# Pairs of 64-row products in both halves of a gated MLP's first matrix product

## Chip, cores and metric

The kernel runs on one core of one Trainium2 chip. The metric is the device time of one execution in microseconds. A core has five engines that run their own instruction streams in program order and wait for each other on semaphores: PE (TensorE, matrix products; its weight loads are listed as PEld), DVE (VectorE), ACT (ScalarE), POOL (GpSimd) and SP (SyncE, which here only issues DMA transfers).

## What is computed

A transformer block on 2048 tokens of width 448: attention with 16 heads, then a gated MLP with a spatial mixing matrix. Both are modulated by vectors made from a condition c. The change lies in the product that makes z.

```python
mod = (_silu(c) @ w_mod).reshape(c.shape[0], 6, 1, -1)      # sa, ca, ga, sb, cb, gb
h = _layernorm(x) * (1 + ca) + sa
x = x + ga * attention(h, wqkv, wo)                          # 16 heads
h = _layernorm(x) * (1 + cb) + sb                            # h2 below
z = _gelu(jnp.einsum("bsd,df->bsf", h, w_in))                # 448 -> 1792
z1 = z[..., :896]                                            # first half
z2 = _layernorm(z[..., 896:])                                # second half
g = jnp.einsum("ts,bsf->btf", w_sp, z2) + b_sp[None, :, None]
x = x + gb * jnp.einsum("bsf,fd->bsd", z1 * g, w_out)
```

## The kernel before

**Number format.** Products run in a reduced fp32 format. To keep precision every operand is split in two: a rounded part, "hi", and the rest, "lo". A product of two matrices is hi x hi + lo x hi + hi x lo. With 448 = 3 x 128 + 64 rows to contract, one output tile takes the eleven full products of `STEPS` (L27 to L30): nine for the three whole blocks of 128 rows, and two for the last 64 rows, `STEPS_Z = [(6, 6), (6, 7)]`. In slot 6 of the activations, rows 0 to 63 hold hi of the last 64 rows and rows 64 to 127 hold their lo; slot 6 of the weights holds hi twice. So (6, 6) is hi x hi and lo x hi in one product. (6, 7) is hi x lo: slot 7 of the weights holds lo in rows 0 to 63, and in the first half of z zeros below (the memset of L1135), so half of that product's rows do nothing.

**Activations.** `h2T[g]` is the modulated, transposed input of row group g: 512 tokens, four groups. Group 0 is transposed on TensorE (`h2_first`). For groups 1 to 3, `h2_stats`, `h2_norm` and `h2_turn` (statistics, normalizing and a blockwise transpose on DVE), `h2_put` (four DMAs to memory, `hs_scr`), `h2_load` (five DMAs back: blocks 0, 2, 1, and the last 64 rows twice) and `h2_group` follow. `h2_group` takes one block: an activation with scale and bias on ACT (L1188), a rounding on ACT (L1189) and a subtraction on DVE (helper `sub`, L151).

**First half of z.** `z1_unit(g, f)` (L1197) makes 128 of the 896 columns for one row group: eleven products of 128 x 128 by 512 into one PSUM bank (L1200), a Gelu on ACT into one of four slots of `zbuf` (L1204), and a DMA of the slot to memory (L1205). The loop over g and f has 28 units, counted n = 7g + f. Behind unit n stand, in program order, the steps of `H2_AT` for later row groups: `h2_load(1)` behind n = 0, `h2_group(1)` behind 3, 4 and 5, the statistics to the put of group 2 behind 0 to 3 and of group 3 behind 4 to 7, `h2_load(2)` behind 5, `h2_load(3)` behind 9, `h2_group(2)` behind 8 to 11, `h2_group(3)` behind 13 to 16. Between them stand the loads and splits of the second half's weights (`win_load`, `win_prep`) and, from n = 10 on, the parts of w_out (`wout_load` behind 10 + 2i, `wout_part` behind 12 + 2i, `wout_store` behind 13 + 2i for part i).

**Second half of z.** `z2_gemm(t)` makes one of sixteen token tiles: two times eleven products of 128 x 128 by 448 (L1453), Gelu (L1460), statistics (L1461). `z2_norm` follows one tile later. For tiles 4 to 15 the (6, 7) product is replaced: `z2_halves` (L1437) runs, three times per run, two products of 64 rows, one on rows 0 to 63 from `h2T[g]`, one on rows 64 to 127 from `twin`, a second copy of hi of the last 64 rows in the lower partitions. The two products of a pair belong to the two column halves and go to two banks. `twin_load` fetches the copy from `hs_scr` and `twin_make` (L1430) modulates and rounds it on ACT, once for each of groups 1 to 3.

**What sets the order.** Everything is placed by hand (`manual_schedule`); each engine runs its instructions in the order of the program text. `bank(name)` (L232) hands out PSUM banks in turn from a list of seven. SP issues nearly all DMAs, one after the other; an issue that has to wait holds back those behind it.

Of the kernel before, what the change touches and what calls it, by code (L numbers as in the profile page):

```python
# [99 lines left out]
def tile_adaln_mha_gmlp(ctx, tc, x, wqkv, wo, w_in, w_spT, b_sp, w_out, cT, w_mod0, w_mod, out):  # L100
# [34 lines left out]
    def hview(heap, off, a, b):  # L135
        return heap[:, off : off + a * b].rearrange("p (a b) -> p a b", b=b)
# [13 lines left out]
    def sub(eng, dst, a, hi):  # L150
        eng.tensor_tensor(out=dst, in0=a, in1=hi.bitcast(F32), op=ALU.subtract)  # L151
# [980 lines left out]
    sub(dve, parts[1], osb[h], parts[0])  # L1132
    for g in range(2):
        x_load(g)
    pool.memset(w1[64:128, 7, :].bitcast(F32), 0.0)  # L1135
# [58 lines left out]

    zbuf = []

    def z1_unit(g, f):  # L1197
        ps_t = bank("z1_ps")
        for j, (a, b) in enumerate(STEPS):
            pe.matmul(ps_t, w1[:, b, f * 128 : (f + 1) * 128], h2T[g][:, a, :], start=j == 0, stop=j == NST - 1)  # L1200
# [3 lines left out]
        act.activation(zt, ps_t, AF.Gelu_apprx_tanh)  # L1204
        sp.dma_start(z1_scr[f * 128 : (f + 1) * 128, g * 512 : (g + 1) * 512], zt)  # L1205

    for t in range(8, 12):
        wo_tile(t)
# [18 lines left out]
    def wout_part(f):  # L1227
        raw = wouts[f][0]
        dve.tensor_tensor(out=raw, in0=raw, in1=bcs["gb"], op=ALU.mult)
        hi, lo = (wo3.tile([128, D], F32R, name=f"wout_{i}") for i in range(2))  # L1230
        act.activation(hi, raw, AF.Copy)
        sub(dve, lo, raw, hi)
        wouts[f] = hi, lo
# [78 lines left out]
    def wouts_load(g):  # L1312
        for at_g, i, f in WOUT_AT:
            if at_g == g:
                if (i, f) == (0, 0):
                    tbuf.append(wp.tile([128, 5120], F32R, name="wouts", tag="tw", bufs=1))
                if (i, f) == (1, 4):
                    tbuf.append(wp.tile([128, 1536], F32R, name="wouts2", tag="once", bufs=1))
# [15 lines left out]
    def z_sum(p):  # L1334
        if p >= NM:
            return
        for d, a, b, op in MIX[p][0]:
            if d == ONCE:
                once[:] = [wp.tile([128, 1536], F32, name="once", tag="once", bufs=1).rearrange("p (t c) -> p t c", c=384)]
# [79 lines left out]

    ph4 = ExitStack()  # L1420
    tz = ph4.enter_context(tc.tile_pool(name="tz", bufs=2))
    z_mv = {}

    twins = {}
    twin = wp.tile([128, NG - 1, 512], F32R, name="twin", tag="once", bufs=1)

    def twin_load(g):
        sp.dma_start(twin[64:128, g - 1, :].bitcast(F32), hs_scr[g - 1][384:D, :])

    def twin_make(g):  # L1430
        twins[g] = twin[:, g - 1, :]
        t = twins[g][64:128]
        act.activation(t, t.bitcast(F32), AF.Identity, scale=cols["cb"][64:128, 3:4], bias=cols["sb"][64:128, 3:4])

    z2_ps = {}

    def z2_halves(ts):  # L1437
        for t in ts:
            g, tt = divmod(t, 4)
            cs = slice(tt * 128, (tt + 1) * 128)  # L1440
            for hf, (src, r) in enumerate(((h2T[g][:, 6, :], slice(0, 64)), (twins[g], slice(64, 128)))):
                z2_ps[t, hf] = bank("z2_ps")
                pe.matmul(z2_ps[t, hf][:, :D], src[r, cs], w2[r, 7, hf * D : (hf + 1) * D], start=True, stop=False)

    def z2_gemm(t):
        g, tt = divmod(t, 4)
        st = tz.tile([128, 2, 6], F32, name="stz")
        for hf in range(2):
            early = (t, hf) in z2_ps
            ps_t = z2_ps.pop((t, hf)) if early else bank("z2_ps")  # L1450
            steps = STEPS[:-1] if early else STEPS
            for j, (a, b) in enumerate(steps):
                pe.matmul(  # L1453
                    ps_t[:, :D],
                    h2T[g][:, a, tt * 128 : (tt + 1) * 128],
                    w2[:, b, hf * D : (hf + 1) * D],
                    start=j == 0 and not early,
                    stop=j == len(steps) - 1,
                )
            act.activation(z2[t][:, hf * D : (hf + 1) * D], ps_t[:, :D], AF.Gelu_apprx_tanh)  # L1460
            dve.bn_stats(out=st[:, hf, :], in_=z2[t][:, hf * D : (hf + 1) * D])  # L1461
        mv = tz.tile([128, 2], F32, name="mvz")
        dve.bn_aggr(out=mv, in_=st)
        rs = tz.tile([128, 1], F32, name="rsz")
        rstd_of(mv[:, 1:2], rs, 1)
        z_mv[t] = (mv, rs)
# [245 lines left out]
```

## Time and profile before

| what | value |
|---|---|
| median of 3 runs | 1366.69 us (1366.53 to 1367.1) |
| the profiled execution: its time, its span | 1367.53 us, 1365.7 us |
| first half of z (L1200), on the chain | from 897.49 us, 69.93 us, 308 products |
| second half of z (L1453, L1443), on the chain | from 967.42 us to about 1037.9 us |
| granted TensorE clock | 1.00 throughout |

A page of the profile tells of one execution. Its span runs from the first to the last instruction; the rest of the time lies around it. The chain of waits follows the work that ended last back through what released it. A timeline row is: start, length, engine, line, operation, out<-in, shape, count, and in brackets the idle time of that engine before it and what ended it. The letter q behind an engine (SPq) stands for its sequencer, which issues DMAs. A windows row is: stretch, its length, busy time and count of PE, PEld, DVE, ACT and POOL, granted clock, DMA share, GB/s. In the list of waits a row is: who waited for whom, total us, times, longest.

### The profile page before, as it was taken

The page shows a single profiled execution, that of the slowest core. Times are in us where ns is not written, and L with a number is a line of the kernel's source. Part 1 is how long each engine was busy: PE and PEld are TensorE (multiplying, and loading weights), DVE is VectorE, ACT ScalarE, POOL GpSimd, SP SyncE. Part 2 cuts the span into 40 slices and gives each one's busy share as a digit, 9 for nine tenths or more (in the row PEclk, how much of TensorE's full clock was granted, in tenths as well). Part 3 has the DMA queues.
Part 4 walks back from the last instruction along what each step waited for, and adds up shares of the span by engine and source line. Part 5 has one row for each costly group of instructions (what it writes and reads, how often), then busy time and mean ns, then how long its engine had stood idle before and what let it go on. Part 6 is the DMA issues. An engine that isn't in the chain of part 4 may idle for free.

```text
span 1365.7 us, 20771 instructions
## 1 busy us (share of the span) xinstructions
PE 1359.4 (100%) x7050; PEld 966.1 (71%) x7050; DVE 1112.2 (81%) x1764; ACT 807.3 (59%) x1478; POOL 361.5 (26%) x370
## 2 busy tenths in 40 slices
PE   9999999999999999999999999999999999999998
PEld 7888665556555555555565554888888888888898
DVE  7898999999999999999999991673467778999752
ACT  6623676777677667766776679556335545555411
POOL 2134434244544355654641002210021000000000
PEclk9999999999999999999999999999999999999999
DMA  8465747777677668787873110578604665787553
GB/s 284 139 175 183 229 127 218 232 212 205 216 228 234 178 207 256 216 226 221 239 226 114 43 44 24 184 219 273 234 31 155 226 199 175 259 288 260 177 165 109
DMA packets 144518, 260.59 MB, mean 191 GB/s; under 512 B 22168, under 2 KB 43034, under 8 KB 141866
## 3 DMA queue, kind: packets, MB, share of 16 engines
q1 hardware_dynamic: 141694, 255.09, 60.3%
q10 hardware_dynamic: 2718, 4.19, 0.8%
q8 instruction: 55, 0.90, 0.3%
q14 instruction: 51, 0.42, 0.1%
HBM read 178.07 MB, written 76.34 MB: 186 GB/s over the span
## 4 chain that ended last, share of the span: by engine, by line
PE 99%; DVE 1%; DMA 0%; issue 0%; POOL 0%; ACTq 0%; DVEq 0%
PE st_ps L745 19%; PE mt L713 17%; PE o_ps L760 17%; PE acc L1528 5%; PE acc L1529 5%; PE acc L1530 5%; PE pq L408 5%; PE z_ps L1200 5%; PE z_ps L1453 5%; PE wo_ps L832 3%; PE pv L390 2%; PE y_ps L1599 2%; PE y_ps L1600 2%; PE y_ps L1601 2%; PE acc L1536 1%; PE acc L1537 1%
## 5 line engine op out<-in xcount | busy, mean ns | idle before, releaser
L718 DVE TENSOR_REDUCE pm<-mt 128x1 f32<-128x512 f32 x1024 | 626.1, 677 | 7.9 <-PE mt L713 7.8
L749 ACT ACTIVATE P<-st_ps 128x512 f32<-128x512 f32 x1024 | 512.0, 648 | 201.3 <-PE st_ps L745 197.8
L745 PE MATMUL st_ps<-qst,kst 128*128 128x512 f32 x1024 | 408.3, 408 | 0.0
L713 PE MATMUL mt<-kst,qst 128*128 128x512 f32 x1024 | 401.3, 392 | 0.0
L745 PEld LDWEIGHTS st_ps<-qst,kst 128*128 128x128 f32 x1024 | 191.3, 188 | 127.8 <-DVE pm L718 53.3
L760 PE MATMUL o_ps<-P,V 128*32 128x512 f32 x2048 | 240.0, 597 | 0.0
L713 PEld LDWEIGHTS mt<-kst,qst 128*128 128x128 f32 x1024 | 192.4, 188 | 35.6 <-ACT P L749 1.1
L870 POOL TENSOR_TENSOR ws_raw<-ws_raw 128x512 f32<-128x512 f32 x112 | 144.1, 1291 | 173.2 <-DMA ws_raw<-in_w_spT_dram 107.4
L1414 ACT ACTIVATE heapB<-raw_sp 128x512 fp32r<-128x512 f32 x156 | 96.8, 630 | 98.5 <-PE acc L1530 71.1
L760 PEld LDWEIGHTS o_ps<-P,V 128*32 128x32 f32 x2048 | 58.9, 109 | 127.3 <-issue 90.9
L1530 PE MATMUL acc<-heapB,heapA 128*128 128x512 f32 x312 | 121.4, 389 | 0.0
L1528 PE MATMUL acc<-heapB,heapA 128*128 128x512 f32 x312 | 121.4, 389 | 0.0
L766 DVE TENSOR_TENSOR osb<-osb,o_ps 128x512 f32<-128x512 f32 x82 | 56.3, 687 | 61.9 <-PE o_ps L760 59.9
L151 DVE TENSOR_TENSOR heapB<-raw_sp,heapB 128x512 fp32r<-128x512 f32 x112 | 74.5, 685 | 28.1 <-ACT heapB L1414 28.1
L1529 PE MATMUL acc<-heapB,heapA 128*128 128x512 f32 x222 | 86.5, 390 | 0.0
L1530 PEld LDWEIGHTS acc<-heapB,heapA 128*128 128x128 f32 x312 | 58.6, 188 | 12.2
L1528 PEld LDWEIGHTS acc<-heapB,heapA 128*128 128x128 f32 x312 | 58.6, 188 | 12.1
L408 PE MATMUL pq<-heapD,heapD 128*128 128x512 f32 x196 | 61.8, 390 | 0.0
L151 POOL TENSOR_TENSOR ws_raw<-ws_raw 128x512 fp32r<-128x512 f32 x44 | 56.7, 1289 | 3.5
L786 POOL TENSOR_TENSOR osb<-osb,rb 128x512 f32<-128x512 f32 x15 | 19.3, 1284 | 110.1 <-DMA rb<-r_scr 89.8
L1529 PEld LDWEIGHTS acc<-heapB,heapA 128*128 128x128 f32 x222 | 41.7, 188 | 8.8 <-DVE heapB L151 0.3
L1460 ACT ACTIVATE z<-z_ps 128x448 f32<-128x448 f32 x32 | 17.4, 543 | 45.5 <-PE z_ps L1453 45.5
(230 smaller groups left out, 1661.2 us busy)
## 6 DMA issues: line engine op xcount, KB each, us to landing
ws_raw<-in_w_spT_dram SPq DMA_DIRECT2D x136, 256.0 KB
ws_scr<-ws_raw SPq DMA_DIRECT2D x112, 256.0 KB
ws_raw<-ws_scr SPq DMA_DIRECT2D x88, 256.0 KB
raw_sp<-ws_scr SPq DMA_DIRECT2D x88, 256.0 KB
raw_sp<-in_w_spT_dram SPq DMA_DIRECT2D x68, 256.0 KB
wl_scr<-ws_raw SPq DMA_DIRECT2D x44, 256.0 KB
kst<-qk_scr SPq DMA_DIRECT2D x45, 224.0 KB
qst<-qk_scr SPq DMA_DIRECT2D x45, 224.0 KB
```

Of the source, the lines that this page charges most:

```text
L151: eng.tensor_tensor(out=dst, in0=a, in1=hi.bitcast(F32), op=ALU.subtract)
L408: pe.matmul(pq, wqk[:, b, m * 128 : (m + 1) * 128], hT[g][:, a, :], start=j == 0, stop=j == NST - 1)
L713: pe.matmul(mt, qst[h % 3][:, t * 128 : (t + 1) * 128], kst[h % 3][:, kb * 512 : (kb + 1) * 512], start=True, stop=True)
L718: dve.tensor_reduce(out=pms[h][:, t, kb : kb + 1], in_=mt, axis=AX.X, op=ALU.max)
L745: pe.matmul(st, kst[h % 3][:, kt * 128 : (kt + 1) * 128], qst[h % 3][:, qb * 512 : (qb + 1) * 512], start=True, stop=True)
L749: act.activation(p, st, AF.Exp, scale=SCALE)
L760: pe.matmul(o[32 * qb : 32 * qb + 32, :], V[:, u % NT, h, :], ptiles.pop((u, qb)), start=u == a, stop=u == e - 1)
L870: pool.tensor_tensor(out=a, in0=a, in1=b, op=ALU.add if W_SUMS[v][2] > 0 else ALU.subtract)
L1414: act.activation(hi, raw[0], AF.Copy)
L1528: pe.matmul(o, zh[:, c], hi, start=p < 2 and kt == 0, stop=False, skip_group_check=p > 1)
L1529: pe.matmul(o, zh[:, c], lo, start=False, stop=False, skip_group_check=p > 1)
L1530: pe.matmul(o, zl[:, c], hi, start=False, stop=kt == 3, skip_group_check=p > 1)
```

## The change

Both halves of z now run the (6, 7) product as pairs of 64-row products.

- First half: per row group, units 0 to 3 run ten products each and leave their banks open. Then come three pairs in a row: for units 0 and 1, 2 and 3 (they close their banks), and for 4 and 5 (they open theirs). Four Gelus and four stores follow. Units 4 and 5 run ten products, unit 6 all eleven. To feed the lower rows, lo is kept in all 128 rows of slot 7 of the weights; the memset goes.
- `twin` now holds the copy as finished hi, loaded from `h2T[g]` itself by a DMA ahead of unit 0 of each row group; it has three slots, and group 3 takes that of group 0. The second half uses what is there and loads groups 0 and 3 again; the activations of `twin_make` go.
- Second half: per row group, tiles 0 and 1 run ten products for each half and stay open; then four pairs in a row, for the group's four tiles; then tiles 2 and 3.
- An eighth bank joins the list. `twin` and the later `once` tile live in a pool of their own, and the two w_out tiles have one buffer each instead of two.

```diff
+    tw = ctx.enter_context(tc.tile_pool(name="tw", bufs=1))
+    twin = tw.tile([128, 3, 512], F32R, name="twin", tag="once")
+
+    def twin_load(g):
+        sp.dma_start(twin[64:128, g % 3, :].bitcast(F32), h2T[g][0:64, 6, :].bitcast(F32))
...
-    pool.memset(w1[64:128, 7, :].bitcast(F32), 0.0)
...
-            sub(eng, w1[0:64, 7, :], wraw[0][0:64, 3, :], w1[0:64, 6, :])
+            sub(eng, w1[:, 7, :], wraw[0][:, 3, :], w1[:, 6, :])
...
-    def z1_unit(g, f):
-        ps_t = bank("z1_ps")
-        for j, (a, b) in enumerate(STEPS):
-            pe.matmul(ps_t, w1[:, b, f * 128 : (f + 1) * 128], h2T[g][:, a, :], start=j == 0, stop=j == NST - 1)
+    def z1_halves(g, fs, start):
+        for f, src, r in zip(fs, (h2T[g][:, 6, :], twin[:, g % 3, :]), (slice(0, 64), slice(64, 128))):
+            if start:
+                z1_ps[f] = bank("z1_ps")
+            pe.matmul(z1_ps[f], w1[r, 7, f * 128 : (f + 1) * 128], src[r, :], start=start, stop=not start)
+
+    def z1_act(g, f):
         if not zbuf:
             zbuf.append(t3.tile([128, 4, 512], F32, name="z1t", tag="x3", bufs=3))
         zt = zbuf[0][:, (7 * g + f) % 4, :]
-        act.activation(zt, ps_t, AF.Gelu_apprx_tanh)
+        act.activation(zt, z1_ps.pop(f), AF.Gelu_apprx_tanh)
         sp.dma_start(z1_scr[f * 128 : (f + 1) * 128, g * 512 : (g + 1) * 512], zt)
+
+    def z1_unit(g, f):
+        if f == 0:
+            twin_load(g)
+        z1_mm(g, f, STEPS if f == 6 else STEPS[:-1], f < 4 or f == 6, f > 3)
+        if f == 3:
+            for fs in ((0, 1), (2, 3), (4, 5)):
+                z1_halves(g, fs, fs[0] == 4)
+            for k in range(4):
+                z1_act(g, k)
+        elif f > 3:
+            z1_act(g, f)
...
+    banks.append(7)
...
-        hi, lo = (wo3.tile([128, D], F32R, name=f"wout_{i}") for i in range(2))
+        hi, lo = (wo3.tile([128, D], F32R, name=f"wout_{i}", bufs=1) for i in range(2))
...
-    banks.sort(key=lambda k: k < 3)
-    for g in range(1, NG):
-        twin_load(g)
+    banks.sort(key=lambda k: k > 2)
+    twin_load(0)
     for t in range(NT + 1):
-        if t in (2, 5, 9):
-            twin_make((2, 5, 9).index(t) + 1)
-        if t in (4, 7, 10, 13):
-            z2_halves(range(t, t + 3))
         if t < NT:
-            z2_gemm(t)
-        if 0 < t <= NT:
+            for hf in range(2):
+                z2_mm(t, hf, STEPS[:-1], t % 4 < 2, t % 4 > 1)
+                if t % 4 > 1:
+                    z2_act(t, hf)
+            if t % 4 > 1:
+                z2_stats(t)
+        if t % 4 == 1 and t < NT:
+            for k in range(4):
+                z2_halves(t - 1 + k, k > 1)
+            if t == 1:
+                twin_load(3)
+            for k in range(2):
+                for hf in range(2):
+                    z2_act(t - 1 + k, hf)
+                z2_stats(t - 1 + k)
+                z2_norm(t - 1 + k)
+        if t % 4 == 3 or t % 4 == 0 and t:
             z2_norm(t - 1)
```

`z1_mm` and `z2_mm` issue the listed steps into a unit's or a tile's bank, with start and stop as given; `z2_act` is Gelu and statistics of one half, `z2_stats` the rest of a tile's statistics.

More of the change, by code (lines that the diff above doesn't have):

```diff
@@ L1195, in tile_adaln_mha_gmlp, with z1_mm @@
     zbuf = []
-    def z1_unit(g, f):
-        ps_t = bank("z1_ps")
-        for j, (a, b) in enumerate(STEPS):
-            pe.matmul(ps_t, w1[:, b, f * 128 : (f + 1) * 128], h2T[g][:, a, :], start=j == 0, stop=j == NST - 1)
+    z1_ps = {}
+    def z1_mm(g, f, steps, start, stop):
+        if start:
+            z1_ps[f] = bank("z1_ps")
+        for j, (a, b) in enumerate(steps):
+            pe.matmul(
+                z1_ps[f],
+                w1[:, b, f * 128 : (f + 1) * 128],
+                h2T[g][:, a, :],
+                start=start and j == 0,
+                stop=stop and j == len(steps) - 1,
+            )
+    def z1_halves(g, fs, start):
+        for f, src, r in zip(fs, (h2T[g][:, 6, :], twin[:, g % 3, :]), (slice(0, 64), slice(64, 128))):
+            if start:
+                z1_ps[f] = bank("z1_ps")
+            pe.matmul(z1_ps[f], w1[r, 7, f * 128 : (f + 1) * 128], src[r, :], start=start, stop=not start)
+    def z1_act(g, f):
         if not zbuf:
@@ L1317, in wouts_load @@
                 if (i, f) == (1, 4):
-                    tbuf.append(wp.tile([128, 1536], F32R, name="wouts2", tag="once", bufs=1))
+                    tbuf.append(tw.tile([128, 1536], F32R, name="wouts2", tag="once"))
                 sp.dma_start((wouts_l if i else wouts_h)(f).bitcast(F32), wo2_scr[i, f])
@@ L1421, in tile_adaln_mha_gmlp @@
     tz = ph4.enter_context(tc.tile_pool(name="tz", bufs=2))
[L1422 to L1433, printed above, removed]
-    z2_ps = {}
@@ L1437, in z2_halves @@
[L1437 to L1441, printed above, removed]
-                z2_ps[t, hf] = bank("z2_ps")
[L1443 to L1461, printed above, removed]
@@ new lines, in tile_adaln_mha_gmlp, with z2_mm @@
+    z_mv, z_st = {}, {}
+    z2_ps = {}
+    def z2_mm(t, hf, steps, start, stop):
+        g, tt = divmod(t, 4)
+        ts, fs = slice(tt * 128, (tt + 1) * 128), slice(hf * D, (hf + 1) * D)
+        if start:
+            z2_ps[t, hf] = bank("z2_ps")
+        for j, (a, b) in enumerate(steps):
+            pe.matmul(
+                z2_ps[t, hf][:, :D],
+                h2T[g][:, a, ts],
+                w2[:, b, fs],
+                start=start and j == 0,
+                stop=stop and j == len(steps) - 1,
+            )
@@ new lines, in z2_halves, with z2_act @@
+    def z2_halves(t, start):
+        g, tt = divmod(t, 4)
+        ts = slice(tt * 128, (tt + 1) * 128)
+        for hf, (src, r) in enumerate(((h2T[g][:, 6, :], slice(0, 64)), (twin[:, g % 3, :], slice(64, 128)))):
+            if start:
+                z2_ps[t, hf] = bank("z2_ps")
+            pe.matmul(z2_ps[t, hf][:, :D], src[r, ts], w2[r, 7, hf * D : (hf + 1) * D], start=start, stop=not start)
+    def z2_act(t, hf):
+        if hf == 0:
+            z_st[t] = tz.tile([128, 2, 6], F32, name="stz")
+        o = z2[t][:, hf * D : (hf + 1) * D]
+        act.activation(o, z2_ps.pop((t, hf))[:, :D], AF.Gelu_apprx_tanh)
+        dve.bn_stats(out=z_st[t][:, hf, :], in_=o)
@@ L1462, in z2_gemm, with z2_stats @@
+    def z2_stats(t):
         mv = tz.tile([128, 2], F32, name="mvz")
-        dve.bn_aggr(out=mv, in_=st)
+        dve.bn_aggr(out=mv, in_=z_st.pop(t))
         rs = tz.tile([128, 1], F32, name="rsz")
```

2 lines of the change are left out of this document (1 added, 1 removed).

## The prediction, made before the changed kernel had run

> **What bounds the kernel now.** I read the page first, then busy time by stage, the chain of waits in order of time, and then each engine's timeline across the stage that makes the first half of z.
>
> ```profile
> span 1365.7 us, 20771 instructions
> PE 1359.4 (100%) x7050; PEld 966.1 (71%) x7050; DVE 1112.2 (81%) x1764; ACT 807.3 (59%) x1478; POOL 361.5 (26%) x370
> ...
> PE 99%; DVE 1%; DMA 0%; issue 0%; POOL 0%; ACTq 0%; DVEq 0%
> ```
>
> TensorE is on the chain for 99% of the span. A product that falls away is therefore worth its spacing on TensorE, if nothing else is late there; a wait that TensorE gains is paid in full.
>
> ```profile
> 897.30:967.30 70.00, 70.00 (x310) 57.80 (x310) 35.64 (x67) 38.84 (x63) 2.45 (x2) 1.00 0.87 275
> 967.30:1037.80 70.50, 70.50 (x354) 63.23 (x353) 41.87 (x82) 24.72 (x41) 13.34 (x15) 1.00 0.23 78
> ```
>
> These are the two stages that change, first half of z and second half: length, TensorE busy, its weight loads, DVE, ACT and POOL, then the granted clock (1.00), the DMA share and GB/s. TensorE has no gap in either. The DMA engines differ: 0.87 busy in the first, 0.23 in the second. A transfer that is late has little room to catch up in the first.
>
> ```profile
> 897.49 69.93 PE z_ps L1200 x308
> 967.42 17.83 PE z_ps L1453 x88
> 985.26 0.81 PE z_ps L1443 x6
> 986.06 12.36 PE z_ps L1453 x60
> 998.43 0.81 PE z_ps L1443 x6
> ```
>
> The chain of waits (start, length, count) gives the prices. A full 512-column product costs 69.93/308 = 0.227 us, a 448-column one 17.83/88 = 0.203. Before already has runs of three pairs (L1443). From one run to the next is 998.43 - 985.26 = 13.17 us for 60 full products and 3 pairs. As 63 slots of 0.203 that would be 12.76, so a pair costs one slot, and **going into a run and out of it costs 0.41 us**.
>
> [...]
>
> **The change: what TensorE saves.**
> - Second half: runs stay four, but hold four pairs instead of three. Four slots go: 4 x 0.203 = **-0.81 us**. Ends: 0 if the four added pairs ran one product after the other, -0.81 as in the old runs; I take the latter, since the product form is that of L1443.
> - First half: 28 products of 64 useful rows ran as full ones. 24 become 12 pairs, 12 slots less: 12 x 0.227 = 2.72; four new runs cost 4 x 0.41 = 1.64. **-1.08 us**, 0.27 a row group. The cost of a run with 512 columns isn't in the trace: between nothing (-2.72) and 0.41 x 512/448 = 0.47 (-0.84). I take the 448-column figure, the nearest row.
>
> Together -1.89 us at most, if TensorE waits nowhere.
>
> **What ACT now does later.** Before, each unit's Gelu ran right behind its products. After, the Gelus of units 0 to 3 stand behind the pairs that follow unit 3, four in a row, and h2_group(1) still stands behind them in program order.
>
> ```profile
> 900.08 1.28 ACT L1204 ACT_TABLE_LOAD   x1 [4.79 <-PE z_ps L1200]
> 901.38 0.60 ACT L1204 ACTIVATE z1t<-z_ps 128x512 f32<-128x512 f32 x1
> ...
> 907.52 0.60 ACT L1204 ACTIVATE z1t<-z_ps 128x512 f32<-128x512 f32 x1 [1.89 <-PE z_ps L1200]
> 908.01 0.81 ACT L1188 ACTIVATE hfull<-heapB,col_sb,col_cb 128x512 f32<-128x512 f32 x1
> ...
> 913.92 0.63 ACT L1189 ACTIVATE heapB<-hfull 128x512 fp32r<-128x512 f32 x1
> ...
> 961.65 1.07 ACT L1204 ACTIVATE z1t<-z_ps 128x512 f32<-128x512 f32 x2
> ```
>
> The load of the Gelu table waits for the first unit's products like the Gelu itself (4.79 us idle on PE, then 1.28). Before, it hides behind unit 1. After, the first Gelu waits for 40 products and a pair: 897.49 + 40 x 0.227 + about 0.35 = 906.9. Then 1.28 of table and four Gelus at 0.48 (two take 1.07, so the second starts 0.48 behind the first): h2_group(1) starts at 910.2, not at 908.01. **2.2 us later.** From there to the last block's rounding at 913.92 ACT is without a gap, so all of it shifts.
>
> [...]
>
> ```profile
> 912.74 0.69 DVE L151 TENSOR_TENSOR heapB<-hfull,heapB 128x512 fp32r<-128x512 f32 x1 [1.16 <-ACT heapB L1189]
> ...
> 916.06 0.69 DVE L151 TENSOR_TENSOR heapB<-hfull,heapB 64x512 fp32r<-64x512 f32 x1
> ...
> PEld z_ps L1200 <- DVE heapB L151: 0.2, 1, 0.2
> ```
>
> The last two blocks of h2T[1] are finished by these subtractions; between them DVE does the next group's statistics. The second ends at 916.75, and the (6,6) product of unit (1,0) needs it: due at 897.49 + 77 x 0.227 + 9 x 0.227 = 917.0. The list of waits shows that weight load waiting 0.2 us for it: **no slack at all**. After, it ends 2.2 later and TensorE comes 0.27 sooner: 2.5 us of stall, **S1 = +2.5**. Ends: 1.2 if the table load ran ahead of the wait, 2.5 as the row has it.
>
> **What SP now does later.** SP issues in order. It issues the loads of h2T[3] ahead of the four Gelu stores of group 1, which now come as one batch behind the pairs of (1,3); before, three of those stores were out long before.
>
> ```profile
> 919.03 1.09 SPq L1205 DMA_DIRECT2D z_scr<-z1t  x2
> 921.60 3.68 SPq L1091 DMA_DIRECT2D hs_scr<-turn  x4
> ...
> 929.24 1.27 SPq L1103 DMA_DIRECT2D heap<-hs_scr  x3
> 930.55 1.09 SPq L1105 DMA_DIRECT2D heap<-hs_scr  x2
> 931.69 0.58 SPq L1205 DMA_DIRECT2D z_scr<-z1t  x1
> 932.37 0.38 SPq L1225 DMA_DIRECT2D raw_out<-in_w_out_dram  x1
> ```
>
> ```profile
> 926.06 0.60 ACT L1204 ACTIVATE z1t<-z_ps 128x512 f32<-128x512 f32 x1 [1.16 <-DMA z_scr<-z1t]
> ...
> 928.77 0.57 ACT L1204 ACTIVATE z1t<-z_ps 128x512 f32<-128x512 f32 x1
> ...
> 930.75 0.69 DVE L151 TENSOR_TENSOR heap<-hfull,heap 64x512 fp32r<-64x512 f32 x1 [0.76 <-ACT heap L1189]
> ```
>
> The put of group 3's turned rows is out at 925.28, and its loads start at 929.24: 4.0 us from issue to use. The first of the four stores then goes at 931.69 at the soonest (as does the store there now), or at 933.9 if the whole chain shifts with S1's 2.2. It lands 4.0 us later (by the put; by the store of 919.03, whose slot the Gelu at 926.06 waited for, 7.0). Gelu (1,4) writes the same slot of the four, waits for that landing, and the last block of h2T[2] stands behind it: 928.77 to 931.44 is 2.67 us. So it is ready at 938.4 to 940.6; before, at 931.44. TensorE wants it at 897.49 + 163 x 0.227 - 2 x 0.27 + 2.5 = 936.45; with the 0.2 that S1 showed, the stall is 2.1 to 4.3. **S2 = +3.2**, the middle, since part of the gap from 921.60 to 929.24 is waiting for earlier transfers, which needn't shift. Below, 0, if a store lands at once; above, 7.4 with the 7.0.
>
> ```profile
> 937.81 0.62 DVE L1229 TENSOR_TENSOR raw_out<-raw_out,bc_gb 128x448 f32<-128x448 f32 x1 [6.37 <-DMA raw_out<-in_w_out_dram]
> 938.47 0.58 ACT L1231 ACTIVATE wout<-raw_out 128x448 fp32r<-128x448 f32 x1 [7.27 <-DVE raw_out L1229]
> ```
>
> The copy of h2T[2]'s 64 rows (twin_load(2)) stands on SP behind the stores of the first w_out part. That part's load takes 5.4 us (932.37 to 937.81) and goes three stores later, 933.9 to 936.1. With the product (0.66), rounding (0.6) and two issues (0.9), the copy is issued at 941.5 to 943.7 and lands 4.0 later, 945.5 to 947.7. TensorE wants it at 936.45 + 3.2 + 31 x 0.227 = 946.7: **S3 = +0.5** (0 to 1.0). The copies of groups 0, 1 and 3 I take as covered by the 40 products (9.1 us) ahead of their pairs; if group 1's is late, S2 shrinks by as much.
>
> **Edits at nothing.**
>
> ```profile
> L1135 POOL MEMSET heapA<- x1: 842/842/842, 862.1 to 862.1; 64x896 f32 x1
> L1433 ACT ACTIVATE twin<-twin,col_sb,col_cb x3: 812/812/812, 977.0 to 1008.1; 64x512 fp32r<-64x512 f32 x3
> ```
>
> The memset and the three activations that go are off the chain. Single wout buffers make each rounding on ACT wait for the store before; that puts the last Gelus near 971, while TensorE needs their banks only some 2 us into the second half: covered, about 3 us if not. The eighth bank and the moved `once` cost nothing that these rows show. In the second half ACT is 24.72 us busy of 70.5, and bursts of four Gelus pass.
>
> **Sum.** -0.81 - 1.08 + 2.5 + 3.2 + 0.5 = **+4.3 us**. The profiled execution took 1367.53 (span 1365.7); the median is 1366.69, 0.84 lower. Moved by the same, the time after is 1366.69 + 4.3 = **1371.0**.
>
> **Rivals.**
> - *All of it hidden*: -1.89, **1364.8**, not slower. It needs the (6,6) product of (1,0) not to wait; decided by whether h2_group(1) starts before about 908. For it: TensorE's rows have no gap. Against: the 0.2 us wait. 12%.
> - *S1 alone*: stores land quickly enough that S2 and S3 vanish; 2.5 - 1.89 = +0.6, **1367.3**. Decided by the first store of group 1 landing before 933.5. For: DMA is freed while SP waits for the Gelus. Against: share 0.87, and the 7.0 us of one store. 21%.
> - *ACT becomes the bound*: rounding through single wout buffers runs late by over 3 us, and banks of the last group aren't free when the second half starts; +3 more, **1374 to 1377**. 9%.
> - *Pairs with 512 columns don't overlap*: the first half gains nothing and loses the 1.64; +7.0, 1373.7. Against: L1443 runs as pairs. 2%.
> - *No cost for a run at all*: -2.72 - 0.81 = -3.5, 1363.2. 2%.
>
> The forecast keeps 54%, with 1369.4 to 1374 of its own. A measurement of this kernel can tell about 0.2% (2.7 us) from no change. Faster by more: 0.03 (the last rival, and 1% of the first). Within: 0.34 (the rest of the first, the second, and 2% of the forecast's lower edge). Slower: 0.63 (all else). The range, 1366.0 to 1375.0, leaves out the hidden case, the last rival and the worst of the third.
>
> **What would show it.** TensorE idle at unit (1,0) for DVE's subtraction, 2 to 3 us; a table load near 907; Gelu (1,4) waiting for a DMA and a second idle of TensorE at (2,0); a short one before group 2's pairs. The second half 0.8 us shorter. If TensorE has no idle in the first half, S1 to S3 are wrong and the time is 1364.8.

## The result, and the profile after

| | before | after |
|---|---|---|
| median of 6 runs each, us | 1366.82 | 1377.18 (1374.73 to 1378.05) |
| ratio after/before, 95% interval (not the quotient of the two medians) | | 1.0072 [1.0062, 1.0082] |
| profiled execution: time, span, us | 1367.53, 1365.7 | 1378.03, 1376.2 |

The change makes the kernel 10.4 us slower: the predicted sign, but 6.2 us more than predicted, and above the range. From the page of after, the span and the shares of the chain:

```profile
span 1376.2 us, 20772 instructions
...
PE 93%; DVE 2%; DMA 2%; SPq 1%; ACT 0%; issue 0%; POOL 0%; POOLq 0%; ACTq 0%; DVEq 0%
```

Part of the chain has left TensorE: DMA and SP's queue stand on it now. Where, the starts of the first product of each stage tell (in the trace, us):

| stage | before | after | difference |
|---|---|---|---|
| up to the first half of z | 897.33 | 896.51 | -0.82 |
| first half of z | 69.93 | 81.46 | +11.53 |
| second half of z | 70.52 | 69.72 | -0.80 |
| mixing to the end | 327.95 | 328.53 | +0.58 |

So nearly everything is lost in the first half. Busy time by stage for after (length; busy us and count of PE, PEld, DVE, ACT, POOL; granted clock, DMA share, GB/s) and the list of waits of its weight loads (sum, times, longest):

```profile
896.70:978.00 81.30, 74.08 (x309) 57.60 (x309) 35.33 (x67) 37.73 (x63) 2.45 (x2) 0.94 0.79 254
...
927.50:932.00 4.50, 4.27 (x13) 3.00 (x14) 0.69 (x1) 3.69 (x6) 0.00 (x0) 0.62 0.36 96
949.50:956.50 7.00, 6.23 (x18) 4.54 (x19) 3.26 (x5) 5.52 (x11) 0.00 (x0) 0.56 0.43 151
```

```profile
PEld z_ps L1220 <- DMA twin<-heap: 3.5, 1, 3.5
PEld z_ps L1220 <- DMA twin<-heapB: 3.3, 1, 3.3
...
PEld z_ps L1208 <- DVE heapB L151: 1.4, 1, 1.4
```

Three waits of over a microsecond in the first half, where before had none of over 0.3 us. Two are the pairs (L1220) waiting for the copy in `twin`, 3.3 us for group 1 and 3.5 for group 2; one is (6, 6) of unit (1,0) waiting for DVE. The windows show a second loss behind the two long waits: **the granted clock is 0.62 and 0.56 there**. For 7 to 11 products in a row the spacing is 0.427 us or more instead of 0.227.

Set product by product against e10 below, the same 308 products without these waits, the excess is 1.3 us at 917, 5.1 from 927.7 to 931.9 (3.3 of wait, 1.8 of slow products), and 6.2 from 950.3 to 955.7 (3.5 and 2.7): 12.6. With the saving of 1.08 that is the +11.5.

Why the copies are late stands in SP's timeline of after (start, length, what, count):

```profile
916.88 1.27 SPq L1109 DMA_DIRECT2D heap<-hs_scr  x3
918.19 2.24 SPq L1111 DMA_DIRECT2D heap<-hs_scr  x2
920.52 0.53 SPq L1117 DMA_DIRECT2D raw_in<-in_w_in_dram  x1
921.15 0.38 SPq L1227 DMA_DIRECT2D z_scr<-z1t  x1
921.58 0.49 SPq L1031 DMA_DIRECT2D twin<-heapB  x1
...
943.76 0.33 SPq L1117 DMA_DIRECT2D raw_in<-in_w_in_dram  x1
944.19 0.38 SPq L1227 DMA_DIRECT2D z_scr<-z1t  x1
944.62 0.96 SPq L1272 DMA_DIRECT2D wo_scr<-wout  x2
945.63 0.91 SPq L1031 DMA_DIRECT2D twin<-heap  x1
```

Group 1's copy is issued at 921.58, behind `h2_load(2)`, whose first load had to wait until the put had landed (916.88), a weight load and a store. TensorE wants it at 924.4 (it resumes at 927.7, less the 3.3 us of waiting). It lands at 927.7, 6.1 us after its issue. Group 2's goes out at 945.63, behind three things: a load of w_in (L1117), which waits for its buffer until DVE's subtraction frees it at 943.73, the store of unit (1,6), and the stores of the first w_out part. From SP's list of waits, and the chain of after (start, length, count):

```profile
SPq L1117 <- DVE heapF L151: 3.8, 1, 3.8
```

```profile
945.63 4.60 DMA twin<-heap
950.23 0.04 issue
950.27 1.65 PE z_ps L1220 x4
```

Ahead of these rows the chain of after has no piece of TensorE back to 906.71, where the Gelus of group 0 start: it runs over the stores of these Gelus, the put and load of h2T[2], the put of h2T[3], SP's issues behind it, and the load of the first w_out part (935.23 to 940.53) with DVE's and ACT's work on it. The wait for group 1's copy lies beside it.

ACT's timeline of after, at the start of the first half:

```profile
895.69 1.28 ACT L1226 ACT_TABLE_LOAD   x1 [1.21 <-DVE turn L1093]
906.22 2.07 ACT L1226 ACTIVATE z1t<-z_ps 128x512 f32<-128x512 f32 x4 [9.25 <-PE z_ps L1220]
908.14 0.83 ACT L1193 ACTIVATE hfull<-heapB,col_sb,col_cb 128x512 f32<-128x512 f32 x1
```

The table load has run ahead of the wait on TensorE: nine idle microseconds stand between it and the first Gelu, instead of in front of it. So `h2_group(1)` starts 11.5 us behind the first product (908.14 less 896.68), and not the 12.7 that I had worked out.

The second half is as priced. Chain of after, from one run of pairs to the next:

```profile
986.25 1.01 PE z_ps L1481 x8
987.25 16.42 PE z_ps L1467 x80
1003.67 1.02 PE z_ps L1481 x8
```

80 full products and four pairs take 17.42 us. As 84 slots of 0.203 that would be 17.0: a run of four pairs costs 0.4 us as well.

### The profile page after: what moved, and what is told of

It reads as the page before. It is cut to its first block, busy times and chain, and to the rows that moved or that the text cites. A ratio compares the mean times of both kernels' runs of the same rounds, so it can differ in the third digit from the quotient of the medians.

```text
span 1376.2 us, 20772 instructions
## 1 busy us (share of the span) xinstructions
PE 1363.3 (99%) x7050; PEld 965.9 (70%) x7050; DVE 1111.2 (81%) x1764; ACT 803.2 (58%) x1475; POOL 357.0 (26%) x369
## 4 chain that ended last, share of the span: by engine, by line
PE 93%; DVE 2%; DMA 2%; SPq 1%; ACT 0%; issue 0%; POOL 0%; POOLq 0%; ACTq 0%; DVEq 0%
PE st_ps L745 19%; PE mt L713 17%; PE o_ps L760 17%; PE pq L408 5%; PE acc L1568 5%; PE acc L1569 5%; PE acc L1567 5%; PE z_ps L1467 3%; PE wo_ps L832 3%; PE z_ps L1208 2%; PE pv L390 2%; PE y_ps L1638 2%; PE y_ps L1639 2%; PE y_ps L1640 2%; PE acc L1575 1%; PE acc L1577 1%
## 5 line engine op out<-in xcount | busy, mean ns | idle before, releaser
L172 POOL TENSOR_TENSOR rsz<-rsz,mhalf 128x1 f32<-128x1 f32 x16 | 10.5, 654 | 123.0 <-DVE rsz L171 123.0
```

## The experiments

Ratios are to the kernel before, in runs on the same chip. Two theories were to be told apart at the outset: that SP's queue order and the DMA made the copies late (the prediction's S3), and that the late Gelus hold the chain of `h2_group` (S1, S2), of which the copies are only the first to show.

**e1_second_half.** The first half as before, the memset put back, the three copies loaded ahead of the second half.

```diff
+    pool.memset(w1[64:128, 7, :].bitcast(F32), 0.0)
...
-        if f == 0:
-            twin_load(g)
-        z1_mm(g, f, STEPS if f == 6 else STEPS[:-1], f < 4 or f == 6, f > 3)
...
+        ps_t = bank("z1_ps")
+        for j, (a, b) in enumerate(STEPS):
+            pe.matmul(ps_t, w1[:, b, f * 128 : (f + 1) * 128], h2T[g][:, a, :], start=j == 0, stop=j == NST - 1)
...
-    twin_load(0)
+    for g in range(3):
+        twin_load(g)
     for t in range(NT + 1):
```

> The changed kernel with the first half of z as before (eleven full products a unit, Gelu behind each unit); the second half, the eight banks and the single w_out buffers stay as changed, and the three copies are loaded at the start of the second half. Theory (the loss is TensorE waiting in the first half for the copies of groups 1 and 2, 3.2 and 3.4 us, a granted clock of one half for some 1.5 and 2.4 us worth of lost time after each wait, and 1.2 for h2T[1]): all of that goes, the second half keeps its -0.8, the start of the mixing keeps its new wait of about 0.6; 1366.6, between 1366.0 and 1367.2, and no gap of TensorE over 1 us. Rival (eight banks, the moved tiles or the second half's bursts cost time): 1369 or more.

Measured: 1367.08 against 1367.12, ratio 0.9999 [0.9991, 1.0008]. The second half takes 69.72 us, 0.80 less; but the mixing starts with a wait of 0.9 us, where before waits 0.3. From the waits of e1's weight loads:

```profile
PEld acc L1565 <- DVE heapB L151: 0.9, 1, 0.9
```

All the loss is in the first half, and the second half's gain is about given back at the start of the mixing, where DVE is still busy with the norms of the last tiles.

**e2_copy_earlier** and **e3_copy_by_pool.** The copies of groups 1 to 3 go out right behind the last block's subtraction (e2); or GpSimd makes all of them, with no DMA at all (e3).

```diff
                 sub(dve, hi[64:128], f[64:128], hi[64:128])
+                twin_load(g)                                         # e2
+                pool.tensor_copy(twin[64:128, g % 3, :], f[64:128])  # e3, and the same in h2_first
...
-        if f == 0:
-            twin_load(g)
+        if g == 0 and f == 0:                                        # e2
+            twin_load(0)                                             # e2
```

> The changed kernel with one DMA moved: the copies of groups 1 to 3 are issued on SP right behind the step that finishes their source, ahead of the next group's loads, instead of ahead of unit 0 of their group. Theory (the copies are late by their place on SP, and their wait hid a second one for h2T[2]'s last block): both waits for copies go and the clock stays at 1.00, TensorE now waits 2 to 3 us at the (6, 6) product of unit (2, 0); 1369 to 1370.5. Same theory without the hidden wait: 1367.2. Rival (the DMA engines are so full that a copy is late from any place): 1374 or more, with waits for copies.

> The changed kernel with no DMA for the copies in the first half: GpSimd rounds the lower 64 rows of the same fp32 block into the copy. Theory: as the run with the copy issued earlier, 1368.5 to 1370.5, with the wait for h2T[2]'s last block and none for a copy. Rival (DMA engines too full): this one is fast, below 1371, while the run with the copy issued earlier stays at 1374 or more. Rival (the waits for copies only stand in for late Gelus or single w_out buffers): it stays above 1374 too.

Measured: 1373.37, ratio 1.0045 [1.0030, 1.0060], and 1373.93, ratio 1.0046 [1.0032, 1.0060]. The waits of their weight loads, e2 first:

```profile
PEld z_ps L1209 <- DVE heap L151: 4.9, 1, 4.9
...
PEld z_ps L1209 <- DVE heapB L151: 1.4, 1, 1.4
```

```profile
PEld z_ps L1211 <- DVE heap L151: 4.6, 1, 4.6
```

No copy is waited for any more, and some 3.5 us come back. In their place stands S2: (6, 6) of unit (2,0) waits 4.6 to 4.9 us for the last block of group 2, and 6 to 10 products behind it run 0.427 apart. The wait is some 2 us longer than I had expected, and I had expected no slow clock behind it; so both times lie about 3 us above their ranges. The copy's way, DMA or engine, hardly matters; the late block does. ACT's waits in e2 name its cause, the fifth Gelu of group 1 waiting for the store that frees its slot:

```profile
ACT z1t L1227 <- DMA z_scr<-z1t: 6.2, 2, 5.9
```

In after that block was late as well. DVE's timeline of after has its subtraction end at 939.27:

```profile
938.58 0.69 DVE L151 TENSOR_TENSOR heap<-hfull,heap 64x512 fp32r<-64x512 f32 x1 [5.41 <-DMA z_scr<-z1t]
```

There TensorE came 5 us late itself, by the copy of group 1, and so waited only 0.2 us for it: one wait covered another. These two runs tell one thing more. TensorE doesn't stop at 924 in them, and yet SP comes at most 0.9 us sooner (1.3 counted from the start of each first half): the first load of h2T[3] goes out at 929.95 (e2) and 929.62 (e3), in after at 930.36; the first load of w_out at 934.55 and 934.54, in after at 935.23; its first store at 943.83 and 943.73, in after at 944.62.

**e4_single_wout.** The kernel before with the change's single w_out buffers.

```diff
-        hi, lo = (wo3.tile([128, D], F32R, name=f"wout_{i}") for i in range(2))
+        hi, lo = (wo3.tile([128, D], F32R, name=f"wout_{i}", bufs=1) for i in range(2))
```

> The kernel before with one edit: one buffer instead of two for each of the two w_out tiles. Theory (the waits of ACT for the store before are covered): 1366.8, within 0.5 either way. Rival (single buffers make ACT late, and with it h2T[3] and the Gelus): 1368.5 or more, with TensorE waiting in the first half of z or at the start of the second.

Measured: 1367.84 against 1367.12, ratio 1.0001 [0.9993, 1.0010], with no wait on TensorE that before hasn't. Alone they cost nothing that the runs can tell.

**e5_last_block_sooner.** e3, with group 2's last block ahead of the Gelu that waits for its slot.

```diff
-        (2, ((8, h2_group, (0,)), (9, h2_group, (2,)), (10, h2_group, (1,)), (11, h2_group, (3,)))),
+        (2, ((8, h2_group, (0,)), (9, h2_group, (2,)), (10, h2_group, (1, 3)))),
```

> The run with the copy made by GpSimd, and one step moved: h2_group(2) for its last block stands behind unit (1, 3) (ahead of the Gelu of (1, 4), which waits for its slot's store) instead of behind unit (1, 4). Theory (that Gelu's wait for its slot holds the block back; TensorE's 4.4 us there and some 1.6 to 2.4 for the clock after it are all of that one wait): both go, the clock is 1.00; what is left is h2T[1]'s 1.2, a mixing start 0.7 to 1 late and perhaps a wait up to 1 for h2T[3]; 1366.7 to 1368. Rival (the block is late because its transfer from memory or ACT's total work is late): the wait moves a little but stays over 2 us; 1371 or more.

Measured: 1369.8, ratio 1.0026 [1.0016, 1.0035]. The wait at (2,0) is gone, so S2's mechanism is shown: moving one block past the store's wait removes it. But the sum missed by about 2 us, since the next hidden wait came out. The waits of e5's weight loads, and ACT's timeline ahead of the first:

```profile
PEld z_ps L1211 <- ACT z1t L1229: 1.6, 1, 1.6
...
PEld z_ps L1211 <- DVE heapB L151: 1.4, 1, 1.4
...
PEld acc L1569 <- DVE heapB L151: 1.2, 1, 1.2
```

```profile
947.44 0.58 ACT L1267 ACTIVATE wout<-raw_out 128x448 fp32r<-128x448 f32 x1 [3.30 <-DMA wo_scr<-wout]
...
952.18 0.58 ACT L1267 ACTIVATE wout<-raw_out 128x448 fp32r<-128x448 f32 x1 [1.41 <-DVE raw_out L1265]
952.66 1.56 ACT L1229 ACTIVATE z1t<-z_ps 128x512 f32<-128x512 f32 x3
```

TensorE, due at 951.8, gets its bank only at 953.3. The four Gelus of group 2 that would free them stand in program order behind two roundings of w_out, and these wait 3.3 us for the store of the part before and 1.41 for DVE's product of the next part.

**c1_idle_2us** and **c2_idle_4us.** Was the slow clock behind the waits caused by the idle time, or by something else in that stage, such as its transfers? The kernel before, with two or six copies of a block onto itself on ACT ahead of tile 8 of the second half, where the DMA engines are quiet (share 0.23 in before); TensorE has to wait for them.

```diff
+        if t == 8:
+            for _ in range(2):      # 6 in c2
+                act.activation(h2T[2][:, 0, :], h2T[2][:, 0, :].bitcast(F32), AF.Copy)
         if t < NT:
             z2_gemm(t)
```

> The kernel before, with TensorE made to idle once in the second half of z, where the DMA engines are little used: ahead of token tile 8 ACT copies one block of h2T[2] onto itself twice, and the tile's first product waits for it. About 2 us of idle. Theory (the granted clock halves after an idle of 3 us or more, whatever it waited for): the idle is paid alone, products follow at 0.20 us, clock 1.00; 1368.8. Rival (any wait of this kind slows the products behind it): products at 0.37 to 0.4 us behind it, 1370 or more.

> As the run with two copies, but six: about 4.5 us of idle. Theory: products at about 0.37 us (448 columns at half the clock) for up to 3.4 us behind it, so 1 to 2 us beyond the idle, and a mean clock under 1.00; 1372.4 to 1373.4. Rival (the slow products of the first half were due to its busy DMA engines): products at 0.20 us at once, 1371.3.

Measured: 1369.28, ratio 1.0020 [1.0010, 1.0030], and 1373.51 (two runs), ratio 1.0050 [1.0031, 1.0068]. The wait that was made, from each run's list, c1 first, then c2:

```profile
PEld z_ps L1453 <- ACT heap L1485: 2.3, 1, 2.3
```

```profile
PEld z_ps L1453 <- ACT heap L1485: 5.0, 1, 5.0
```

Busy time by stage right behind the idle time in c1; then in c2, idle time and what follows:

```profile
1005.00:1010.00 5.00, 5.00 (x24) 4.57 (x25) 0.99 (x3) 1.10 (x3) 0.76 (x1) 1.00 0.17 62
```

```profile
1003.00:1008.00 5.00, 0.42 (x3) 0.04 (x1) 1.64 (x4) 4.32 (x7) 0.91 (x1) 0.73 0.30 107
1008.00:1013.00 5.00, 4.99 (x15) 4.52 (x16) 0.27 (x1) 0.55 (x1) 0.00 (x0) 0.58 0.00 0
```

After a gap of 2.3 us the clock stays at 1.00. After one of 5.0 it is 0.58, and eleven products take about 2 us more than their 0.203 each. The DMA share is 0.30 in that idle time and 0.00 behind it. So the wait of 5.0 us cost its length and some 2 us beyond, and it took no busy DMA engines for that. The theory's 3.4 us at half clock are what after has behind its first long wait (0.62 over 4.5 us: 4.5 x 0.38 / 0.5), but they are no upper end: behind the second it is at least 4.7 (0.50 from 950.3 to 955.0), and in c2 5.0 x 0.42 / 0.5 = 4.2.

**e7_all_mended.** e5, with the blocks of group 1 a unit sooner, the last three of group 3 together behind n = 14, and the last norm of z2 behind the first rounding in the mixing (its row stands under e11). Where steps of groups 1 and 2 stand behind the same unit, those of group 2 now come first.

```diff
-        (1, ((0, h2_load), (3, h2_group, (0, 2)), (4, h2_group, (1,)), (5, h2_group, (3,)))),
         (2, ((0, h2_stats), (1, h2_norm), (2, h2_turn), (3, h2_put), (5, h2_load))),
+        (1, ((0, h2_load), (2, h2_group, (0, 2)), (3, h2_group, (1,)), (4, h2_group, (3,)))),
...
-        (3, ((13, h2_group, (0,)), (14, h2_group, (2,)), (15, h2_group, (1,)), (16, h2_group, (3,)))),
+        (3, ((13, h2_group, (0,)), (14, h2_group, (2, 1, 3)))),
```

> The run before this one with three more moves: h2_group(1) one unit sooner (behind units 2, 3, 4), h2_group(3)'s last two blocks behind unit (2, 0), and the normalizing of the last token tile behind the split of the mixing's third weight block. Theory (the pairs save the predicted 1.89 us and every loss was a wait behind a late step): no wait of TensorE over 0.3 us in the first half, none new at the start of the mixing; 1365.0, between 1364.4 and 1366.0. Rival (the pairs with 512 columns save less than predicted): 1366.5 or more without any wait.

Measured: 1372.03, ratio 1.0039 [1.0026, 1.0053]: a miss, and slower than e5. The waits at (1,0) and at the mixing are gone. In the waits of e7's weight loads stand one for a bank and three for blocks, and ACT's timeline shows what is late:

```profile
PEld z_ps L1211 <- ACT z1t L1229: 4.2, 1, 4.2
PEld z_ps L1211 <- DVE heap L151: 1.8, 3, 1.2
```

```profile
907.98 0.63 ACT L1196 ACTIVATE heapB<-hfull 128x512 fp32r<-128x512 f32 x1
908.63 1.28 ACT L1229 ACT_TABLE_LOAD   x1
909.92 2.07 ACT L1229 ACTIVATE z1t<-z_ps 128x512 f32<-128x512 f32 x4
...
955.48 0.58 ACT L1267 ACTIVATE wout<-raw_out 128x448 fp32r<-128x448 f32 x1 [2.07 <-DMA wo_scr<-wout]
955.97 2.04 ACT L1229 ACTIVATE z1t<-z_ps 128x512 f32<-128x512 f32 x4
```

The blocks of group 1 now stand ahead of the Gelus, and so ahead of the table load. ACT's idle time (10.65 us, until the loads land at 905.76) lies in front of these blocks and no longer hides the load; the Gelus come 3.7 us later than in after. The Gelus of group 2 start at 955.97, 3.3 us later than in e5 and still behind w_out; TensorE waits 4.2 us for a bank and the clock drops again (0.998 as the mean of the profiled run, 1.00 in e10).

**e8_double_wout, e9_double_and_moved, e10_wout_later.** Is it w_out's single buffers that hold ACT, or its place? e8 is e5 with two buffers of each kind in the same space: lo is written over the loaded tile. e9 adds two orders: group 3's statistics on DVE two units sooner, out of the way of group 1's last block, and e7's place for the last norm. e10 has these two orders, but single buffers, and each step of w_out one unit later.

```diff
-        hi, lo = (wo3.tile([128, D], F32R, name=f"wout_{i}", bufs=1) for i in range(2))
+        hi, lo = wo3.tile([128, D], F32R, name="wout_0"), raw.bitcast(F32R)             # e8, e9
...
+        (3, ((2, h2_stats),)),                                                          # e9, e10
-        (3, ((4, h2_stats), (5, h2_norm), (6, h2_turn), (7, h2_put), (9, h2_load))),
+        (3, ((5, h2_norm), (6, h2_turn), (7, h2_put), (9, h2_load))),
...
-            for fn, n in ((wout_load, 10), (wout_part, 12), (wout_store, 13)):
+            for fn, n in ((wout_load, 11), (wout_part, 13), (wout_store, 14)):          # e10
```

> The kernel of e5_last_block_sooner, with the w_out parts double-buffered in the same space: the low part is written in place over the loaded tile, so that two high and two loaded tiles of 1792 bytes stand where two loaded and one of each part stood. If ScalarE is held by the single buffers (a rounding waits until the stores of the block before have landed, and the Gelus behind it come late), the 1.75 us wait for a bank near 953 goes and the time is 1.5 to 2.5 us below e5's 1369.8 - about 1367.5 to 1368.3, with the 1.4 us wait at (6,6) of (1,0) and the late start of the mixing left. If the rounding itself, not its wait, is what stands before the Gelus, the bank wait stays above 1 us and the time is 1369.3 to 1370.

> e8 with two orders mended: the statistics of group 3 issued behind unit 2 instead of unit 4 (so that the last low part of group 1 is not behind them on VectorE), and the last norm of z2 issued behind the first rounding of w_spatial's blocks in the mixing. If the waits found so far are all there is, what is left is the saving of the change itself, 1.9 us: 1365.0 (1364.3 to 1366). If waits go on to move to another place, a gap of over 1 us shows on TensorE and the time is 1366.5 to 1369.

> As e9, but with the change's single w_out buffers, and each step of w_out (load, rounding, store) one unit later, so that only one rounding stands before the four Gelus of group 2 instead of two. If the place of the roundings is what matters: no wait for a bank over 1 us and 1365 to 1366.5. If the single buffers hold ScalarE wherever the roundings stand, a bank wait of 1.5 to 4 us at group 1, 2 or 3 and 1367 to 1371.

Measured: e8 1374.41, ratio 1.0046 [1.0031, 1.0062]; e9 1371.8, 1.0028 [1.0017, 1.0040]; e10 **1365.8, 0.9988 [0.9979, 0.9997]**. In e8 the wait for a bank is still there (PEld). ACT's waits from 930 to 960 and SP's from 940 to 972 tell why: the roundings wait 7.6 us for tiles that are loaded late, and the loads wait on SP for the store of lo from the same tile. In e5 the roundings waited 5.2 us for stores and 3.7 for DVE's products.

```profile
PEld z_ps L1468 <- ACT z1t L1229: 3.6, 2, 2.6
PEld z_ps L1211 <- ACT z1t L1229: 1.6, 1, 1.6
```

```profile
ACT wout L1267 <- DVE raw_out L1265: 7.6, 3, 3.7
```

```profile
SPq L1261 <- DMA wo_scr<-raw_out: 13.1, 5, 4.0
```

e8 fell out as neither theory had it: 3.6 us more of waiting for banks at the start of the second half, behind which the clock drops as well (0.62 from 974.5 to 979.0). It is the same cause once more. Ahead of the last group's four Gelus (968.97) ACT stands at two roundings, 3.4 and 4.0 us long:

```profile
968.49 0.58 ACT L1267 ACTIVATE wout<-raw_out 128x448 fp32r<-128x448 f32 x1 [4.00 <-DVE raw_out L1265]
```

e9, with w_out in its old place, still waits 3.4 us for a bank near 954, and 1.8 at the start of the second half; its time lies above both of its ranges. e10, which differs from e9 in w_out's place and buffers, waits for none near 954, and the wait at (1,0) is gone in both. So the later place takes the wait at group 2 away, and single buffers don't bring it back. What two independent buffers at the old place would do, e8 and e9 don't show, since their loads wait for a store. All waits of TensorE that e10 has left from the first half to the start of the mixing, "issue" apart, and its first half:

```profile
PEld z_ps L1469 <- ACT z1t L1229: 1.4, 2, 1.1
```

```profile
896.70:965.60 68.90, 68.90 (x310) 55.00 (x309) 34.63 (x65) 35.38 (x60) 3.86 (x5) 1.00 0.83 257
```

The 1.4 us are the price of the later place: at the start of the second half TensorE waits for a bank whose Gelu stands behind one more rounding of w_out. e5 and e7, with single buffers at the old place, have no such wait.

```profile
969.31 0.58 ACT L1267 ACTIVATE wout<-raw_out 128x448 fp32r<-128x448 f32 x1 [1.90 <-DMA wo_scr<-wout]
```

So e10's second half takes 71.14 us, not 69.72. By stage it differs from before by -0.84 up to the first half, -1.08, +0.62 and, mixing to the end, -0.42 us.

**e11_second_half_mended.** e1, with the last norm of z2 moved as in e7, e9 and e10.

```diff
-        if t % 4 == 3 or t % 4 == 0 and t:
+        if t % 4 == 3 or t in (4, 8, 12):
             z2_norm(t - 1)
...
         w_split(g + 2)
+        if g == 0:
+            z2_norm(NT - 1)
```

> The kernel of e1_second_half (first half as before the change, second half with the runs of four pairs) with the last norm of z2 issued behind the first rounding of w_spatial's blocks. If the second half's saving of 0.8 us was given back at the start of the mixing, the wait of 0.91 us there falls to about 0.3 and the time is 0.6 to 0.9 us below the kernel before: ratio 0.9994 to 0.9996. Then the pairs of the first half carry the rest of e10's gain (its ratio is 0.9988). If the norm's place doesn't matter, the time is that of the kernel before.

Measured: 1366.15 against 1366.89, ratio 0.9996 [0.9987, 1.0005]. The wait at the mixing falls as expected:

```profile
PEld acc L1565 <- DVE heapB L151: 0.4, 2, 0.2
```

The time is 0.74 us lower, which the interval can't tell from none; the rows of the trace (second half 69.72 us, mixing to the end 328.04) carry it better than the runs do.

## Why the prediction was wrong

The sign, the stage and the kind of loss (TensorE waiting for steps that come late) were right; the sum was 6.2 us short, and the three waits didn't fall as it had them. By its own steps:

- *Second half, -0.81*: right, -0.80.
- *First half, -1.08, from the 448-column price of a run*: right. In e10 the first half takes 68.85 us from its first product to that of the second half, 1.08 less than before's 69.93. Six slots around each of its four runs of three pairs (the first from 905.34 to 907.13) take 1.78 to 1.79 us: 0.42 to 0.43 more than six of 0.227.
- *S1, +2.5*: the wait is there, at its low end. 1.3 instead of 2.5, because the table load ran ahead of the wait. The prediction had named that as its other end, and took the row of before.
- *S2, +3.2*: right as a mechanism. In e2 and e3 the wait is 4.6 to 4.9, above the 2.1 to 4.3 that it was the middle of and below the outer end of 7.4; it is gone when the block is moved (e5). In after it is 0.2, for the reason given: "if group 1's is late, S2 shrinks by as much". That half-sentence became the main case.
- *"The copies of groups 0, 1 and 3 I take as covered by the 40 products"*: **this step failed**. The 40 products of cover begin when the unit begins; the copy begins when SP gets to it. For group 1 I never worked out that time. SP stood behind `h2_load(2)`, and even with the shorter landing of before, 4.0 us, the copy would have come at 921.58 + 4.0 = 925.6, not at 924.4. With the 6.1 that it took, the wait is 3.3. But this wait stood where S2 would have stood, and didn't set the time: the chain passes it by, and in e2 and e3, without it, SP's steps up to the w_out stores come at most 1.3 us sooner. With that copy in time, TensorE would have waited longer further on. This is read from these rows; no run moves group 1's copy alone.
- *S3, +0.5 (0 to 1.0)*: right place, but **the step that set the time, and it failed by its size**: the wait is 3.5. The load of the first w_out part was issued within the forecast range, at 935.23, and took 5.3 us instead of 5.4. From its landing to the copy's issue the step counted a product, a rounding and two issues, 2.2 us. It took 5.1 (940.53 to 945.63), since SP was held until 943.73 by the load of w_in that waits for its buffer, and then issued a store of z1t first. The landing took 4.6 us, not 4.0.
- *No term for what a wait costs beyond its length*: this **failed** too; the sum took a stall as its length. The slow products behind the two long waits cost 1.8 and 2.7 us. c1 and c2 show that this comes with the idle time: nothing beyond at 2.3 us, about 2 at 5.0.
- *Edits at nothing*: single w_out buffers cost nothing in before (e4). The rival *ACT becomes the bound* didn't decide after, but it was real: once the waits ahead of it are mended, ACT stands behind w_out's roundings and TensorE waits for banks, in the first half (e5, e7, e8, e9) or, as the rival has it, at the start of the second (e8, e9, e10). The start of the mixing, 0.6 us, was in no step at all: with the second half 0.8 us shorter, DVE's last norms became the later ones (e11 moves one of them, and the wait falls to 0.4 in all).

The 6.2 us come out so. When group 2's copy landed, TensorE was 9.9 us behind e10 (1.3 + 5.1 + 3.5), where the prediction had 2.5 + 3.2 + 0.5 = 6.2: 3.7 more. The slow products behind that wait add 2.7 and the mixing 0.6; the stage up to the first half, 0.8 shorter, takes its part off again. That the forecast 6.2 lies near the 8.1 of the three waits in the profile (3.3 + 3.5 + 1.3) is luck: they are other waits.

What stays open: the two halves' savings were never in one run without waits, the first half's in e10 and the second half's in after, e1, e5, e7 and e11. Up to the first half the profiles differ by 1.6 us (896.45 in e2 to 898.05 in e4), and those of before, c1, c2 and e4, whose instructions are the same up to there, by 1.2 among themselves. So 0.84 of e10's 1.7 us between the profiled spans isn't ascribed to the change. And the two w_out buffers of before beside the change's `twin` were not tried.

## What to carry to other kernels

When a change bunches the instructions that free slots and banks, follow every queue that stands behind them up to the time at which TensorE wants the result; "covered by 40 products" holds only from the moment the transfer is issued (here 2.8 us before TensorE came for it, and it took 6.1). What a transfer waited for on its queue here was everything issued ahead of it, also a load that waited 3.8 us for a buffer. In a stage without slack one mended wait shows the next: here copy, last block, bank. The first half's 1.08 us came only with all of them gone, and then 1.4 us of waiting stood at the start of the second half. So the waits of a profile don't add up to what mending them brings; the chain tells which one sets the time. A stall of TensorE of the lengths seen here, 2.5 us and more, should be priced with some 2 us on top for the clock (1.5 to 2.7 in eight waits).

## What the runs showed of the hardware

- **The clock after a wait.** Starts of products 1.0 to 1.8 us apart (after, e2, e3, e5, e7, e8, e9, e10) and 2.3 apart (c1) left the spacing of the next products as it was. All eight that were 2.5 us apart or more (2.5 in e8, 3.5 to 5.0 in after, e2, e3, e7, e9 and c2) were followed by 6 to 11 slow products, 0.427 us apart with 512 columns and 0.373 with 448, and losses of 1.5 to 2.7 us. In after the granted clock was 0.50 there (928.5 to 930.0 and 951.0 to 953.0). The slow products don't always begin with the first: in e9 they begin 1.0 us behind the wait. The slow stretches lasted 3.1 to 5.5 us. The 3 us of c1's theory would fit the waits of after (1.4 without slow products, 3.3 and 3.5 with them), but they aren't the bound: in e8 a wait of 2.5 us was enough, with one of 1.0 us that began 3 us ahead of it. Whether that earlier wait had a part in it the runs don't tell.
- **Where a table load waits.** The load of the Gelu table ran at 895.69 in after, ten microseconds ahead of the Gelu, and at 908.63 in e7, right in front of it. In before it waited for TensorE's products like the Gelu (4.79 us, then the load at 900.08); in after only the Gelu itself did (9.25 us). The load of 1.28 us was hidden or paid by which of the waits stood in front of it; what decides that, these rows don't show.
- **A run of pairs** costs 0.42 to 0.43 us with 512 columns (e10) and 0.40 to 0.41 with 448 (after, before): the way in and out hardly grew with the columns.
